# Retention attention and a top-1 expert layer on one core: expert weights loaded late and one at a time, and the work at the seam in a new order

## The chip, the cores and the metric

The kernel runs on one core of a Trainium2 chip. The core has TensorE (matmuls and transposes, into PSUM), VectorE, ScalarE and GpSimd for elementwise work, and SyncE, which here only issues transfers; 16 transfer engines are shared by all queues. The metric is the device time of one execution in microseconds, the median of three runs.

## The reference

For 8 batches, 8 heads, 576 tokens and a head size of 64 it computes retention (scores times a decay, causal, without softmax), puts the heads side by side to rows of 512, and sends each row through the one expert of eight that its gate picks:

```python
scores = scale * np.matmul(q, k.transpose(0, 1, 3, 2))
gamma = 1.0 - 2.0 ** (-5.0 - np.arange(H))
ret = scores * Dmat                     # gamma ** (i - j) for i >= j, else 0
attn = np.matmul(ret, v)
x = attn.transpose(0, 2, 1, 3).reshape(B * S, H * D)      # 4608 rows of 512
logits = x @ w_gate                                        # 8 experts
expert_idx = np.argmax(logits, axis=1)
gate_w = softmax(logits)[np.arange(N), expert_idx]
for e in range(E):
    mask = expert_idx == e
    h = np.maximum(x[mask] @ w1[e], 0.0)                   # 512 -> 1024
    out[mask] = gate_w[mask, None] * (h @ w2[e])           # 1024 -> 512
```

Everything comes and goes as float32.

## The kernel before

**Attention.** The tokens of a batch are cut into four blocks of 128 (c = 0 to 3) and one of 64 (c = 4), 40 blocks `i` in all. The main loop runs over them, and the order in which it is written is the order on every engine. The decay is put into k and q: `scale_k` and `scale_q` (mostly GpSimd) write `kk` and `qq`; `stage_T` transposes both on TensorE, ScalarE copies them to `kT` and `qT`. `stage_SC` makes a block's scores in the two PSUM tiles `pssc` as upper-triangle halves, and VectorE masks them into `sc`; `stage_S` adds a block to the running state `pss`, which `stage_se` copies to `se`; `stage_AV` (inside the block) and `stage_IN` (from the state) make the block's output in `psx`, which ScalarE copies to `xT` (line 429). `stage_xb` and `stage_R` turn it back to rows in bf16, and `put_rows` writes them to the DRAM tensor `x_rows`. A block's stages are spread over the loop: block `i` is scored while block `i+2` is transposed. SyncE issues, in the loop's order, k eight blocks ahead, v eight blocks ahead, q a batch ahead and the rows; a load waits for a mark of the loop (`after`) and for its buffer (`ldk` 6, `ldv` 8).

**Routing.** One batch later `stage_L1` and `stage_L2` make the gate's logits, and `route_batch` (VectorE, a generator that the loop advances by `steps`) finds each row's expert, its place among that expert's slots, and the gate weight, which `put_gates` and `write_gates` write beside the row. Each expert has 640 slots: `CA` of them (phase 0) for tokens of the first batches, `CB` (phase 1) for the others. `make_slots(0)` makes the lists of phase 0 as soon as half of the batches are placed, `make_slots(1)` the rest at the end.

**Experts.** A phase of an expert gathers its rows by indirect transfers of 128 rows (`gather`, GpSimd), transposes them (`trans`), multiplies by w1 (`mm1`, ReLU on ScalarE) and by w2 (`mm2`, times the gate on VectorE), and scatters 128 rows at a time to the output (GpSimd). The phases run as `seq`: phase 0 of the first `NA` experts, then their phase 1, then both phases of each further expert. After each ReLU or group of ReLUs, and after each scatter, `on` is called; the first calls carry the rest of the last batch's routing (`script`). Weights come in 64 parts of 0.52 MB, eight an expert, by casting transfers that GpSimd issues (`load_w`): `early` says how many at which block, and `fetch` takes the next ones. Five parts follow the attention loop, six come with the third phase and four with each phase after it. Experts below `EW` have buffers of their own; the others' buffers lie where the attention's were.

## Time and profile before

| what | value |
|---|---|
| median of 3 runs | 348.36 us (346.74 to 349.30) |
| profiled execution, its own time | 348.43 us |
| its span, first to last instruction | 346.7 us |
| mean granted clock of TensorE | 0.989 |
| busy: TensorE, ScalarE, GpSimd, VectorE | 314.7, 184.5, 201.0, 134.2 us |
| moved by the transfer engines | 65.98 MB, mean 190 GB/s |

The prediction sums against the profiled execution's own time, which is its span and what lies around it. The attention ends near 184 us, the experts fill the rest.

### The profile page before, as it was taken

How to read it: one execution, taken by the hardware profiler on the slowest of the kernel's cores; microseconds unless marked ns; L12 is line 12 of the kernel's file. 1: busy time of each engine (PE TensorE's matmuls, PEld its weight loads, DVE VectorE, ACT ScalarE, POOL GpSimd, SP SyncE). 2: the span in 40 equal slices, each digit the busy share in tenths (PEclk: the TensorE clock that was granted, in tenths of full speed). 3: DMA queues.
4: the chain of work that ended last, by engine and by line, in shares of the span. 5: the costliest groups of instructions: out<-in, count | busy, mean ns of one | idle time of the engine just before them, and what ended most of it. 6: DMA issues, size and time to landing. Idle time of an engine off the chain costs nothing. (4 is left out here: it accounts for less than half of the span.)

```text
span 346.7 us, 12050 instructions
## 1 busy us (share of the span) xinstructions
PE 314.7 (91%) x5099; PEld 231.4 (67%) x5115; DVE 134.2 (39%) x412; ACT 184.5 (53%) x371; POOL 201.0 (58%) x257
## 2 busy tenths in 40 slices
PE   6998999979989898997879998999999999999991
PEld 5777887768878787876767664455656465565650
DVE  5432446454564646654463622211212121221211
ACT  4467685655757667475555435355353535354440
POOL 3476755544445552647930287887886887865322
PEclk9999999999999999999998999999999999999997
DMA  8998989989999999996999159898999799953112
GB/s 206 216 236 206 245 204 212 253 202 242 218 227 223 232 225 219 253 198 145 190 203 182 44 145 215 187 207 187 229 200 211 139 208 222 208 163 117 58 58 79
DMA packets 117321, 65.98 MB, mean 190 GB/s; under 512 B 88590, under 2 KB 109582, under 8 KB 117264
## 3 DMA queue, kind: packets, MB, share of 16 engines
q0 software_dynamic: 18432, 31.80, 44.2%
q1 hardware_dynamic: 98304, 33.37, 41.5%
q8 instruction: 41, 0.67, 0.8%
q14 instruction: 16, 0.13, 0.1%
q10 hardware_dynamic: 528, 0.02, 0.1%
HBM read 67.45 MB, written 15.53 MB: 239 GB/s over the span
## 5 line engine op out<-in xcount | busy, mean ns | idle before, releaser
L757 ACT ACTIVATE ht<-pm 128x384 bf16<-128x384 f32 (+1 forms) x96 | 50.5, 527 | 58.7 <-PE pm L62 41.2
L290 POOL TENSOR_TENSOR kk<-kt,kg 128x512 f32<-128x512 f32 x39 | 40.8, 1046 | 59.4 <-PE pss L62 32.2
L62 PE MATMUL py<-w2b,ht 128*128 128x512 bf16 (+1 forms) x312 | 74.0, 374 | 1.1 <-DMA out_dram<-ys,tids 0.2
L62 PE MATMUL pm<-xt,w1b 128*128 128x256 bf16 (+1 forms) x512 | 73.1, 300 | 0.9 <-ACT xt L742 0.9
L915 DVE TENSOR_SCALAR ys<-py,gsl 128x512 f32<-128x512 f32 (+1 forms) x41 | 30.2, 737 | 105.1 <-PE py L62 76.1
L918 POOL DMA_INDIRECT out_dram<-ys,tids x40 | 40.9, 1022 | 48.5 <-DVE s L599 13.8
L62 PEld LDWEIGHTS <-w1b 128*128 128x128 bf16 x512 | 49.8, 98 | 23.3 <-issue 1.3
L384 DVE TENSOR_TENSOR sc<-pssc,mask 128x512 f32<-128x512 f32 x64 | 41.2, 685 | 28.9 <-PE pssc L62 26.6
L62 PEld LDWEIGHTS <-ht 128*128 128x128 bf16 x328 | 30.6, 98 | 30.5 <-ACT ht L757 1.1
L697 POOL DMA_INDIRECT xg<-x_rows,tidg x40 | 41.3, 1032 | 11.9 <-issue 11.2
L62 PE MATMUL psx<-sc,vt 128*64 128x128 f32 (+1 forms) x640 | 38.9, 265 | 1.2 <-issue 0.9
L62 PE MATMUL pssc<-qT,kT 64*64 64x64 f32 (+1 forms) x1024 | 36.1, 256 | 3.2 <-issue 1.7
L280 POOL TENSOR_TENSOR qq<-qt,qg 128x512 f32<-128x512 f32 x28 | 29.7, 1062 | 15.3 <-DMA qt<-in_q_dram 14.6
L323 ACT COPY kT<-pst 128x512 f32<-128x512 f32 x40 | 23.5, 587 | 22.3 <-PE pst L65 18.9
L429 ACT COPY xT<-psx 128x512 f32<-128x512 f32 x32 | 18.8, 587 | 30.1 <-PE psx L62 22.6
L742 ACT COPY xt<-pt 128x512 bf16<-128x512 bf16 x40 | 22.8, 587 | 20.3 <-PE pt L65 12.1
L62 PEld LDWEIGHTS psx<-sc,vt 128*64 128x64 f32 (+1 forms) x640 | 30.8, 136 | 2.5 <-issue 1.6
L62 PEld LDWEIGHTS pssc<-qT,kT 64*64 64x64 f32 x1024 | 27.6, 133 | 7.0 <-ACT xr L475 2.9
L475 ACT COPY xr<-pssc 128x512 bf16<-128x512 bf16 (+1 forms) x38 | 22.6, 596 | 9.6 <-PE pssc L65 9.5
L258 POOL DMA_DIRECT2D w2b<-in_moe_w_dram x32 | 24.3, 781 | 3.0 <-DMA w2b<-in_moe_w_dram 2.3
L62 PE MATMUL pss<-vt,kk 128*64 128x64 f32 x512 | 22.7, 227 | 2.2 <-issue 2.2
L62 PEld LDWEIGHTS pss<-vt,kk 128*64 128x64 f32 x512 | 18.1, 137 | 4.4 <-issue 2.6
(128 smaller groups left out, 373.9 us busy)
## 6 DMA issues: line engine op xcount, KB each, us to landing
kt<-in_k_dram SPq DMA_DIRECT2D x32, 256.0 KB, 5.5
qt<-in_q_dram SPq DMA_DIRECT2D x16, 512.0 KB, 5.5
vt<-in_v_dram SPq DMA_DIRECT2D x32, 256.0 KB, 5.4
w1b<-in_moe_w_dram POOLq DMA_DIRECT2D x32, 256.0 KB
w2b<-in_moe_w_dram POOLq DMA_DIRECT2D x32, 256.0 KB
x_rows<-xr SPq DMA_DIRECT2D x32, 128.0 KB, 5.4
kt<-in_q_dram SPq DMA_DIRECT2D x8, 128.0 KB, 5.7
kt<-in_k_dram SPq DMA_DIRECT2D x8, 128.0 KB, 4.8
```

The source lines that it names most:

```text
L62: nc.tensor.matmul(out=out, lhsT=lhsT, rhs=rhs, start=start, stop=stop, skip_group_check=True)
L258: after(nc.gpsimd.dma_start(out=wb[e][part // n][:, o:o + m, :], in_=w[e, o * P:(o + m) * P, :].rearrange("(c p) f -> p c f", p=P)), dep)
L280: eng.tensor_tensor(out=qq[:, :, :].rearrange("p s (h d) -> p h s d", d=DH), in0=qts[b][:, h0:h0 + 2, :, :], in1=qg[:, 0:NCH, h0:h0 + 2].r ...
L290: eng.tensor_tensor(out=kk[:, :, :], in0=kts.pop(i)[:, :, :], in1=kg[:, blocks[i][1], :].unsqueeze(2).to_broadcast([P, H, DH]), op=ALU.mult)
L323: mark["kT"] = nc.scalar.copy(out=kT[:, :, :].rearrange("p a (u t) -> p u a t", u=2), in_=ps[:, :, o:o + 256].rearrange("p u (a t) -> p u ...
L384: mark["sc"] = nc.vector.tensor_tensor(out=sc[:, j, :, :], in0=pssc[j][:, :].rearrange("p (a i) -> p a i", i=P), in1=mask[:, :].unsqueeze( ...
L475: nc.scalar.copy(out=xr[0:m, :].rearrange("p (a t) -> p a t", t=P), in_=ps)
L697: nc.gpsimd.indirect_dma_start(out=xg[:, :], out_offset=None, in_=x_rows[0:nr, :], in_offset=bass.IndirectOffsetOnAxis(ap=slots[ph][1][:, ...
L742: nc.scalar.copy(out=xts[(e, ph)][:, :, j * P:(j + 1) * P], in_=pt[:, :, :])
L757: nc.scalar.activation(out=ht[:, f0:f0 + per, :], in_=pm[:, :, :], func=AF.Relu)
L915: nc.vector.tensor_scalar(out=ys[:, r], in0=py[:, r], scalar1=gsl[:, e, slots[ph][2] + j:slots[ph][2] + j + 1], scalar2=None, op0=ALU.mult)
L918: scatters.append(nc.gpsimd.indirect_dma_start(out=next(outs)[:, :], out_offset=bass.IndirectOffsetOnAxis(ap=slots[ph][0][:, e, j:j + 1], ...
```

## The change

- **Sizes.** Phase 0 takes 384 slots of the first five batches (`BA`) instead of 256 of the first four, phase 1 has 256 instead of 384; `NA` and `EW` go from 3 to 2.
- **Loads at the start.** The first 128 rows of q of batch 0 are loaded and transposed alone (`qc0`, `first_TQ`); the other 384 rows come after k(1) and v(0); batch 1's q comes after the second block's scores and is scaled and transposed in the last two blocks of batch 0, in part on VectorE and through `scr`. q of later batches is issued at c = 0 and 2 instead of 1 and 3, ahead of k. k is loaded nine blocks ahead and v seven (seven buffers each).
- **Scores.** A batch's first block is scored in full 128 by 128 tiles, and the clearing of `pssc` at the start is gone.
- **Order.** At c = 4 the copies `stage_se` and `stage_xb` come behind the scores and the output stage. One row copy (`NB - 3`) goes to VectorE.
- **Weights.** Nothing is loaded before the last batch; there one part comes with each block, five after the loop, one with each of the calls 0 to 5, and then one with every second call from 8 on. Of experts 2 to 7 the four parts of w2 are loaded by SyncE as float32 into a staging tile, each behind the last ReLU, and cast by VectorE eight or more calls later.
- **Second layer's rows.** w2 parts are read so that a partition holds two neighbouring rows. The first layer's columns are taken with a step of two to match.
- **Routing and seam.** The gathers of phase 0 come one a block from the second block of the last batch on; the last batch's gates are computed and written sooner; gate writes of the last three batches cover exactly their own rows; the script's steps lie at calls 0, 1, 2, 4 and 8, and one of expert 0's transposes lies inside `stage_L1`. GpSimd drains once before the last expert.

```diff
-CA = 256
-CB = 384
+CA = 384
+CB = 256
...
-NA = 3
-EW = 3
+NA = 2
+EW = 2
+BA = 5
...
-    ldk = p1.enter_context(tc.tile_pool(name="ldk", bufs=6))
-    ldv = p1.enter_context(tc.tile_pool(name="ldv", bufs=8))
+    ldk = p1.enter_context(tc.tile_pool(name="ldk", bufs=7))
+    ldv = p1.enter_context(tc.tile_pool(name="ldv", bufs=7))
...
+    qc0 = attc.tile([P, H, DH], F32, name="qc0")
     load_k(0)
-    load_q(0, 0)
-    load_q(0, 1)
-    for i in range(5):
-        load_k(i + 1)
-        load_v(i)
-        if i % 2:
-            load_q(1, i // 2)
+    nc.sync.dma_start(out=qc0[:, :, :], in_=q[0, :, 0:P, :].rearrange("h p d -> p h d"))
+    load_k(1)
+    load_v(0)
+    qts[0] = ldq.tile([P, H, NCH, DH], F32, tag="q", name="qt")
+    for g in range(2):
+        hs = slice(g * NP, (g + 1) * NP)
+        nc.sync.dma_start(out=qts[0][:, hs, 0:NCH - 1, :],
+                          in_=q[0, hs, P:NCH * P, :].rearrange("h (p s) d -> p h s d", p=P))
+    load_k(2)
+    load_v(1)
+    load_k(3)
+    load_v(2)
+    load_k(4)
...
-                                  in_=w[e, o * P:(o + m) * P, :].rearrange("(c p) f -> p c f", p=P)), dep)
+                                  in_=w[e, o * P:(o + m) * P, :].rearrange(
+                                      "(c p) f -> p c f" if part < n else "(p c) f -> p c f", p=P)), dep)
...
+            n = 1 if c == 0 else 2
             for p in range(NP):
-                for u in range(2):
+                for u in range(n):
                     for j in range(2):
                         r = slice(j * DH, (j + 1) * DH)
-                        mm(pssc[j][u * DH:(u + 1) * DH, p * P + u * DH:(p + 1) * P], kT[r, p, u * DH:(u + 1) * DH],
+                        m = slice(u * P // n, (u + 1) * P // n)
+                        mm(pssc[j][m, p * P + u * DH:(p + 1) * P], kT[r, p, m],
                            qT[r, p, c * P + u * DH:(c + 1) * P], True, True)
...
+            if a == 1:
+                between()
...
+        if b == B - 1:
+            yield from gates(b, ex)
+            put_gates(b)
...
-        if b == B // 2:
+        if b == BA:
...
+        n = NCOL if b < B - 3 else NCH
+        o = x_rows[b * S:b * S + n * P, DW:XW].rearrange("(t p) u -> p t u", p=P)
+        todo_g.append((o, gat[:, b * NCOL:b * NCOL + n, :]))
+        if n < NCOL:
+            todo_g.append((x_rows[b * S + n * P:(b + 1) * S, DW:XW], gat[0:REM, b * NCOL + n, :]))
...
-        per = 2 if ph == 0 else 1
+        per = 512 // n
...
-                    mm(pm[:, o, :], w1b[:, c, fb * P:(fb + 1) * P], xt[:, c, :], c == 0, c == NPT - 1)
-            nc.scalar.activation(out=ht[:, f0:f0 + per, :], in_=pm[:, :, :], func=AF.Relu)
+                    mm(pm[:, o, :], w1b[:, c, fb // 2 * 2 * P + fb % 2:fb // 2 * 2 * P + 2 * P:2], xt[:, c, :],
+                       c == 0, c == NPT - 1)
+            mark["mm"] = nc.scalar.activation(out=ht[:, f0:f0 + per, :], in_=pm[:, :, :], func=AF.Relu)
...
-    early = {i: 1 if i < NB - NCOL else 2 for i in (*range(10, 32, 3), *range(NB - NCOL - 1, NB))}
-
-    def fetch(n):
+    early = {NB - 5: 1, NB - 4: 1, NB - 3: 1, NB - 2: 1, NB - 1: 1}
+
+    staged = []
+
+    def fetch(n, call=0):
         for e, j in [wq.pop(0) for _ in range(min(n, len(wq)))]:
-            load_w(e, j, 4, wpool if e < EW else wpool2)
+            if e < EW or j < 4:
+                load_w(e, j, 4, wpool if e < EW else wpool2)
+            else:
+                st = stg.tile([P, 2, DM], F32, tag="st", name="st")
+                after(nc.sync.dma_start(out=st[:, :, :], in_=moe_w2[e, (j - 4) * 2 * P:(j - 3) * 2 * P, :]
+                                        .rearrange("(p c) f -> p c f", p=P)), mark["mm"])
+                staged.append((call, e, j - 4, st))
+
+    def cast_staged(call):
+        if staged and staged[0][0] + 8 <= call:
+            _, e, j, st = staged.pop(0)
+            nc.vector.tensor_copy(out=wb[e][1][:, 2 * j:2 * j + 2, :], in_=st[:, :, :])
...
+        if b == B - 1 and c > 0:
+            gather_first(1)
         fetch(early.get(i, 0))
-        load_k(i + 8, mark.get("sc"))
-        stage_T(i + 2, b + 1, c - 1 if c > 0 and b + 1 < B else None)
-        if c in (1, 3) and b + 2 < B:
-            load_q(b + 2, c // 2, mark.get("kT"))
+        if c in (0, 2) and b + 2 < B:
+            load_q(b + 2, c // 2, mark.get("sc"))
+        load_k(i + 9, mark.get("sc"))
...
+        if c < NCH or i == NB - 1:
+            stage_se()
...
+        if c == NCH and i < NB - 1:
+            stage_se()
+            stage_xb(i - 1)
+        load_v(i + 7, mark.get("xT"))
...
+    gather_first(len(first))
+    fetch(5)
...
-    script = [lambda: stage_L2(B - 1), lambda: (stage_R(NB - 1), put_rows()), turn, None, turn,
-              None, None, None, turn, lambda: make_slots(1)]
+    script = {0: lambda: stage_L2(B - 1), 1: turn, 2: lambda: (stage_R(NB - 1), put_rows()), 4: turn,
+              8: lambda: (turn(), make_slots(1))}
+    calls = iter(range(1000))
     last.append(True)
 
     def on(i):
 
-        f = script.pop(0) if script else None
-        if f:
-            f()
+        n = next(calls)
+        script.get(n, lambda: None)()
         write_gates()
         gather_upto(i + 2)
+        cast_staged(n)
+        if n < 6 or n > 7 and n % 2 == 0:
+            fetch(1, n)
...
+    stg = p2.enter_context(tc.tile_pool(name="stg", bufs=5))
...
-        fetch((EW * 8 - sum(early.values()), 0, 6)[i] if i < NA else 4)
...
+        if i == len(seq) - 2:
+            nc.gpsimd.drain()```

Three places show the new order. First SyncE at the start of the program, before and then after (`kt`, `vt`, `qt` are k, v and q in SBUF, `qc` the single piece of q; of a row the shape is partitions by the rest):

```order
L121 DMA kt<-in_k_dram 128x8x64
L115 DMA qt<-in_q_dram 128x4x256 x2
L121 DMA kt<-in_k_dram 128x8x64
L121 DMA vt<-in_v_dram 128x8x64
L121 DMA kt<-in_k_dram 128x8x64
L121 DMA vt<-in_v_dram 128x8x64
L115 DMA qt<-in_q_dram 128x4x256
L121 DMA kt<-in_k_dram 128x8x64
L121 DMA vt<-in_v_dram 128x8x64
L134 DMA kt<-in_q_dram 64x8x64
```

```order
L122 DMA kt<-in_k_dram 128x8x64
L153 DMA qc_118<-in_q_dram 128x8x64
L122 DMA kt<-in_k_dram 128x8x64
L122 DMA vt<-in_v_dram 128x8x64
L159 DMA qt<-in_q_dram 128x4x192 x2
L122 DMA kt<-in_k_dram 128x8x64
L122 DMA vt<-in_v_dram 128x8x64
L122 DMA kt<-in_k_dram 128x8x64
L122 DMA vt<-in_v_dram 128x8x64
L135 DMA kt<-in_q_dram 64x8x64
```

The rest of the first q moved behind k(1) and v(0), and the half of the second batch's q (the seventh row before) is gone from this stretch.

Second GpSimd in the third batch's blocks, before and then after (`kk` and `qq` are the scaled k and q):

```order
L258 DMA w1b<-in_moe_w_dram 128x1024
L280 TENSOR_TENSOR qq<-qt,qg 128x2x4x64
L290 TENSOR_TENSOR kk<-kt,kg 128x512
L280 TENSOR_TENSOR qq<-qt,qg 128x2x4x64
L290 TENSOR_TENSOR kk<-kt,kg 128x512
L280 TENSOR_TENSOR qq<-qt,qg 128x2x4x64
L290 TENSOR_TENSOR kk<-kt,kg 128x512
L258 DMA w1b<-in_moe_w_dram 128x1024
```

```order
L299 TENSOR_TENSOR qq<-qt,qg 128x2x4x64
L309 TENSOR_TENSOR kk<-kt,kg 128x512
L299 TENSOR_TENSOR qq<-qt,qg 128x2x4x64
L309 TENSOR_TENSOR kk<-kt,kg 128x512
L299 TENSOR_TENSOR qq<-qt,qg 128x2x4x64
L309 TENSOR_TENSOR kk<-kt,kg 128x512 x2
```

The weight parts, one every third block, are gone from between the scalings.

Third GpSimd from the end of the attention into the first experts, before and then after (`xg` are gathered rows, `out_dram` scatters, `tidg` the gather lists of the two phases):

```order
L258 DMA w2b<-in_moe_w_dram 128x2x512 x3
L258 DMA w1b<-in_moe_w_dram 128x1024 x4
L258 DMA w2b<-in_moe_w_dram 128x2x512 x4
L918 DMA out_dram<-ys,tids_3139 4608x512 x2
L697 DMA xg<-x_rows,tidg_4290 128x272 x3
L918 DMA out_dram<-ys,tids_3139 4608x512 x2
L258 DMA w1b<-in_moe_w_dram 128x1024 x4
L258 DMA w2b<-in_moe_w_dram 128x2x512 x2
L697 DMA xg<-x_rows,tidg_4290 128x272 x3
```

```order
L762 DMA xg<-x_rows,tidg_3528 128x272 x2
L272 DMA w2b<-in_moe_w_dram 128x1024 x3
L272 DMA w1b<-in_moe_w_dram 128x1024 x4
L272 DMA w2b<-in_moe_w_dram 128x1024 x4
L1035 DMA out_dram<-ys,tids_3527 4608x512
L762 DMA xg<-x_rows,tidg_4175 128x272 x2
L272 DMA w1b<-in_moe_w_dram 128x1024
L1035 DMA out_dram<-ys,tids_3527 4608x512 x2
L272 DMA w1b<-in_moe_w_dram 128x1024
L762 DMA xg<-x_rows,tidg_4175 128x272 x2
```

The gathers of phase 1 moved ahead of the second scatter, and the six weight parts that stood together ahead of the next gathers became single ones; w2 is no longer among them.

## Rows read from the trace of the kernel before

**Rows 1.** The page, parts 1 and 2: busy time, and DMA in 40 slices.

```profile
PE 314.7 (91%) x5099; PEld 231.4 (67%) x5115; DVE 134.2 (39%) x412; ACT 184.5 (53%) x371; POOL 201.0 (58%) x257
...
DMA  8998989989999999996999159898999799953112
```

**Rows 2.** Busy time by stretch (us from the span's start, cut at xT copies).

```profile
core 0: us, PE busy (x) PEld busy (x) DVE busy (x) ACT busy (x) POOL busy (x), PEclk, DMA share, GB/s
36.20:55.78 19.58, 19.08 (x511) 16.45 (x515) 11.18 (x35) 13.74 (x30) 12.64 (x18) 1.00 0.98 222
55.78:79.36 23.58, 20.19 (x516) 16.84 (x520) 11.69 (x37) 13.73 (x29) 12.03 (x13) 1.00 0.96 219
79.36:100.77 21.41, 19.77 (x516) 16.84 (x520) 11.63 (x36) 13.73 (x29) 9.81 (x10) 1.00 1.01 228
100.77:121.21 20.44, 19.26 (x516) 16.66 (x520) 11.63 (x36) 13.74 (x30) 10.76 (x11) 1.00 1.06 232
121.21:141.87 20.66, 19.37 (x516) 16.75 (x520) 12.41 (x40) 13.73 (x30) 10.04 (x11) 1.00 0.99 220
141.87:166.11 24.24, 21.17 (x529) 17.60 (x533) 11.73 (x36) 13.73 (x30) 14.54 (x17) 1.00 0.90 200
166.11:184.68 18.57, 15.81 (x374) 13.28 (x370) 11.04 (x37) 10.65 (x22) 10.06 (x14) 0.92 1.11 195
184.68:234.49 49.81, 46.95 (x329) 28.93 (x330) 15.74 (x56) 22.70 (x43) 31.31 (x36) 0.99 0.77 161
234.49:328.52 94.03, 92.14 (x611) 56.42 (x620) 20.28 (x50) 45.23 (x85) 66.85 (x75) 1.00 0.81 178
328.52:346.70 18.18, 10.64 (x64) 6.16 (x63) 3.22 (x5) 3.93 (x8) 4.18 (x5) 0.88 0.18 67
```

**Rows 3.** Timeline of GpSimd: two of the eight weight parts in the loop.

```profile
51.52 0.77 POOL L258 DMA_DIRECT2D w1b<-in_moe_w_dram  x1
...
64.16 0.61 POOL L258 DMA_DIRECT2D w1b<-in_moe_w_dram  x1
```

**Rows 4.** Timeline of the start, in order of time.

```profile
4.02 0.69 DVE L290 TENSOR_TENSOR kk<-kt,kg 128x512 f32<-128x512 f32 x1 [0.63 <-DMA kt<-in_k_dram]
...
10.78 1.27 PE L62 MATMUL pssc<-qT,kT 64*64 64x128 f32 x32
...
15.10 1.09 PE L62 MATMUL pssc<-qT,kT 64*64 64x128 f32 x32
...
15.65 1.04 POOL L290 TENSOR_TENSOR kk<-kt,kg 128x512 f32<-128x512 f32 x1 [2.85 <-DMA kt<-in_k_dram]
...
19.24 1.04 POOL L290 TENSOR_TENSOR kk<-kt,kg 128x512 f32<-128x512 f32 x1 [1.52 <-DMA kt<-in_k_dram]
...
36.20 0.59 ACT L429 COPY xT<-psx 128x512 f32<-128x512 f32 x1 [0.81 <-PE pss L62]
```

**Rows 5.** The page, part 3, and groups by line of GpSimd's issues.

```profile
q0 software_dynamic: 18432, 31.80, 44.2%
...
L697 POOL DMA_INDIRECT xg<-x_rows,tidg x40 | 41.3, 1032 | 11.9 <-issue 11.2
...
L258 POOL DMA_DIRECT2D w2b<-in_moe_w_dram x32 | 24.3, 781 | 3.0 <-DMA w2b<-in_moe_w_dram 2.3
...
L258 POOL DMA_DIRECT2D w1b<-in_moe_w_dram x32 | 19.0, 625 | 0.0
```

**Rows 6.** Timeline of TensorE among the experts.

```profile
217.38 0.40 PE L65 MATMUL pt<-identb,xg 128*128 128x128 bf16 x4 [2.00 <-DMA xg<-x_rows,tidg]
...
320.90 3.66 PE L62 MATMUL pm<-xt,w1b 128*128 128x256 bf16 x32
...
328.52 5.36 PE L62 MATMUL pm<-xt,w1b 128*128 128x384 bf16 x32
```

**Rows 7.** Weight loads of TensorE: a group by line, and a timeline row.

```profile
L62 PEld LDWEIGHTS <-w1b 128*128 128x128 bf16 x512 | 49.8, 98 | 23.3 <-issue 1.3
...
8.05 1.36 PEld L65 LDWEIGHTS scr<-ident 128*128 128x128 f32 x7
```

**Rows 8.** Groups by line: VectorE's longest bf16 write from f32.

```profile
L640 DVE TENSOR_TENSOR rh<-scr,r 128x640 bf16<-128x640 f32 x8 | 6.3, 784 | 0.0
```

## What the change was predicted to do

> **What bounds the kernel now.** I read the page first, then the span cut at its stages. The page [rows 1] shows one engine near full all the way: TensorE is busy for 314.7 of 346.7 us, every other engine for less than 60%. The slices below show that the transfer engines are just as full for the first two thirds: DMA stands at 8 or 9 tenths in nearly every slice while the attention runs, falls to 1 in the slice from 191 us, and fades after 310 us. So there are two bounds, and the cut [rows 2] tells which holds where.
>
> The first six rows of [rows 2] run from the copy of a batch's first block to that of the next batch's. In each TensorE has the same 516 matmuls to do (511 and 529 records at the two ends), so equal work takes 19.58, 23.58, 21.41, 20.44, 20.66 and 24.24 us. In the shortest TensorE is busy for 19.08 us, in the others for 19.26 to 21.17 with more idle time; DMA is at 0.90 to 1.06 and 200 to 232 GB/s in all six. Attention is thus held by both: TensorE can do a batch in some 19.2 us, and the transfers add what they add. A batch moves q, k and v (3.54 MB) and its rows (0.59 MB), 4.13 MB, 18.6 us at the 222 GB/s of the first row. What comes on top are weights for the experts, a part every 12 us or so [rows 3].
>
> The experts are different. From 234.49 to 328.52 us TensorE is busy for 92.14 of 94.03 us [rows 2], five experts at 18.81 us each, and DMA has 0.81. Nothing but fewer matmuls would shorten that. Ahead of the batches lies a start that waits for loads; between batches and experts a seam (166.11 to 234.49): in its first part TensorE idles 2.8 us and has a granted clock of 0.92, so some of it runs at 1.2 instead of 2.4 GHz, and in its second DMA is not full (0.77).
>
> The span splits into 36.20 (start) + 129.91 (six batches) + 18.57 (last batch and seam) + 49.81 (first experts) + 94.03 + 18.18 = 346.70 us. The profiled execution took 348.43 us, 1.73 more than its span, and lies at the median of the three runs (348.36), so I sum against it. About 1% is what a measurement of this kernel tells from no change.
>
> **The start.** Before, SyncE queues all of the first batch's q behind k(0), and the next batch's q in two halves among the first batch's blocks. GpSimd's scaling of k(3) and k(4) waits for its load by 2.85 and 1.52 us [rows 4]. The first scores begin at 10.78 us, the second block's at 15.10, and the first block of the second batch is copied at 36.20. After, a q piece of 128 rows is loaded alone, so the first scores need 0.52 MB and not 1.3. But the second block's scores still need k(0), all of q, k(1) and v(0) in front of them: 1.83 MB, 8.3 us at 222 GB/s. k(0), 0.26 MB, was in use at 4.02 us, 2.8 us after such a rate would have it, so the last q lands near 11.1 us; a scaling (1.06 on GpSimd), transposes (0.4) and two copies (0.59 each) put the second scores at some 13.4-13.7 us. From there the old kernel needed 21.1 us to the copy at 36.20. Half of the next batch's q (0.52 MB, 2.4 us of transfers) has left the queue ahead of k(3), so the wait of 2.85 us falls to 0.45; the wait of 1.52 for k(4) follows a scaling of q that has left these blocks too, and I halve it. The next batch's q is now transposed in two blocks instead of four, half of it by whole tiles: 0.8 us more. That gives 21.1 - 2.4 - 0.8 + 0.8 = 18.7, and with 13.6 the copy at 32.3 us: **-3.9**. Bounds: -1.5 (only the earlier scores count) and -6 (the added 0.8 lies beside other work, and both waits go whole).
>
> **The six batches.** Eight weight parts leave the loop (blocks 10 to 31, every third); none comes in. What a part costs the transfers: the queue that GpSimd feeds (q0) has 44.2% of 16 engines' span, 153.2 us, for 64 parts and 80 indirect transfers [rows 5]. The last 18.18 us hold five scatters and almost nothing else, at a share of 0.18 [rows 2]: 3.3 us, 0.65 each. 80 of them are 52 us, and (153.2 - 52)/64 = 1.58 us a part, an estimate. Two parts in a batch are 3.2 us over 18.6 us that TensorE's 19.2 nearly equals. The one row that had almost no weight in it (its only part was issued at 51.52, 4 us before its end [rows 3]) took 19.58 us; the next five averaged 22.07. The sixth of them also had four of the gathers and three of its four parts issued by GpSimd at its end. I take 19.8 a batch, just above the row without weights: 118.8, **-11.1**. Lower bound 19.2 (TensorE's own work), -14.7; upper bound 21.1, the mean of the first five as they are, -3.3. The smaller edits fall in here: the first block's scores in 8 full matmuls instead of 16 halves, q issued two blocks sooner and ahead of k, and the copies at the fifth block behind the scores, so that VectorE no longer waits for ScalarE there. Together they may give 0.2 us a batch, which I leave inside the 19.8. k is loaded one block further ahead and v one block less; at 3.9 us a block seven blocks are 27 us of lead, and I cost that at nothing.
>
> **Last batch and seam.** Weights start in the last batch, one a block, and gathers with them, one a block from the second on; GpSimd has no scaling left by then and runs on without TensorE, so the sixteen parts of the first two experts are all issued before the eighth call of the first expert: at 0.6 to 0.8 us each plus six gathers of 1.03, about 17 us of issuing. TensorE is idle for 2.8 of 18.57 us there [rows 2]. Expert 0's last transpose now lies inside the router's matmuls, one row copy has moved to VectorE. I take **-0.6** (0 to -1.5).
>
> **The first experts.** Phase 0 is now 384 tokens of five batches for two experts, not 256 of four for three: before the late tokens are needed TensorE has two phases of 11 us instead of three of 7.6, some 22 us in both cases. The second gather list is made at the ninth call instead of the tenth, and calls in a 384 phase are shorter (0.65 us against 0.9), some 4 us sooner. Before, TensorE waited 2.00 us for a gather that stood behind six weights issued together [rows 6]; single weights and the earlier list take that away. The routing's own matmuls stay. **-1.5** (+1.5 to -3). Largest fill of an expert, counted from the inputs: 619 of 640 slots, so the slow branch stays shut.
>
> **Steady experts and end.** 40 blocks, the same matmuls; 0. Two things are new. The first layer's weights are read with a step of two columns, 512 loads. No row shows such a load. The packed ones are listed at 98 ns each [rows 7] and hide under the matmuls, which run every 114 ns at 256 columns and some 165 at 384 (3.66 and 5.36 us for 32 [rows 6]); the dearest loads of 128 columns are f32 ones, seven in 1.36 us, 194 each [rows 7]. So the ends are 0 and 256 x (194 - 114) + 256 x (194 - 165) = +27.9 us. I take 0, because the step moves the same 128 two-byte elements and the nearest row by type is the packed one. The Trainium skill, *TensorE: Matmul & The Clock Gate*, on weight-path modes, says the fast load holds for column steps up to 1,024 elements; by that the sum stays, and no run here shows it yet. The other new thing: 24 parts of the second layer come by SyncE as f32 and VectorE casts them, 128x1024 each. The nearest VectorE row is 128x640 f32 to bf16 in 784 ns [rows 8]: 1.25 us each, four an expert, 5 us of VectorE's 18.81, where it is busy for 20.28 of 94.03 us now [rows 2]. An eviction waits for a cast at most 1.25 us; there are two output banks and 1.95 us a block, so TensorE does not see it. GpSimd loses 24 issues of 0.78 us [rows 5].
>
> **Sum.** 32.3 + 118.8 + 18.0 + 48.3 + 94.0 + 18.2 = 329.6, with 1.73 outside the span **331.3 us**.
>
> **Rivals.** *The pace is not the weights'.* q, k, v and rows alone fill 18.6 us, and shares of 0.96 to 1.06 do not follow the weights (two parts in the 23.58, two in the 20.44). Then batches stay at 21.1: 348.4 - 3.9 - 3.3 - 2.1 = 339. Chance 0.16. *Late weights become the wait.* From the ninth call 48 parts come in 94 calls of 1.106 us, 104 us (17 calls an expert); they and some 55 indirect transfers need 48 x 1.58 + 55 x 0.65 = 112. The transfers then end 8 us late, a cast waits for its part, and the evictions behind it on VectorE hold TensorE: 339. Chance 0.11. *Stepped columns are slow to load*, slower than before: it decides once a load takes more than some 173 ns, where both matmul widths have eaten the 17 us; at 194 ns 359 us. Chance 0.07. *GpSimd becomes the bound*: the casts hold it off. It has 4 x 0.62 + 10 x 1.03 = 12.8 us of issuing an expert, 17.8 with the casts added, which fits in 18.81; only casts of twice that price make it late, 4 us an expert for six: 355. Chance 0.03. The rule behind that one is the Trainium skill's, *SBUF — State Buffer*, where an f32 copy on VectorE keeps GpSimd from writing descriptors; no row here shows or denies it.
>
> **How the numbers follow.** Forecast (322 to 338) 0.60, the rivals 0.16, 0.11, 0.07, 0.03, unseen harm 0.03. Lower bounds together: 348.4 - 6 - 14.7 - 1.5 - 3 = 323.2. Upper: 348.4 - 1.5 - 3.3 + 1.5 = 345.1. I say 322 to 345. Faster by over 1% (under 344.9) 0.83, within 1% 0.07, slower 0.10.
>
> **What would show it.** The second batch's first copy near 32 us; batches of 19 to 20 us with DMA below 0.97; no wait of TensorE for a gather; the first layer's loads still near 98 ns; 18.8 us an expert. Wrong if batches stay above 21 us, if VectorE's casts wait for transfers, or if the first layer's 32 matmuls take over 5.5 us at 256 columns.

## The result, and the profile after

The changed kernel takes 328.53 us (median) against 348.76 for the kernel before on the same chip: a ratio of 0.9425, 95% interval 0.9366 to 0.9484. The prediction was 331.3 us in a range of 322 to 345. The profiled execution took 328.53 us, 1.73 more than its span, as before. The chip now and then has a slower spell in which a run takes over 1.5% longer than the kernel's fastest; the ratios leave such runs out, but the profiles of five experiments (weights back in the loop, weights late and single, the old split, no drain, all second-layer parts by GpSimd) are of such runs.

The page of the changed kernel, parts 1 and 2, against [rows 1]:

```profile
PE 310.5 (95%) x4965; PEld 231.5 (71%) x4981; DVE 152.6 (47%) x437; ACT 184.1 (56%) x371; POOL 185.1 (57%) x235
...
DMA  9999998899998999965999499999999999973121
```

TensorE is busy for 4.2 us less, in a span 19.9 us shorter: most of what went away is its idle time, 32.0 us before and 16.3 now.

The span of the changed kernel cut as in [rows 2], but the experts cut where an expert ends (three, then five), then the last scatter:

```profile
core 0: us, PE busy (x) PEld busy (x) DVE busy (x) ACT busy (x) POOL busy (x), PEclk, DMA share, GB/s
34.52:54.46 19.94, 18.90 (x495) 16.61 (x499) 11.18 (x35) 13.81 (x29) 12.93 (x21) 1.00 1.02 225
54.46:74.93 20.47, 19.41 (x500) 16.92 (x504) 11.76 (x37) 13.81 (x29) 9.24 (x9) 1.00 0.96 239
...
134.29:153.50 19.21, 19.09 (x503) 16.82 (x506) 11.86 (x39) 13.71 (x29) 8.60 (x9) 1.00 0.72 161
153.50:170.69 17.19, 15.24 (x388) 12.78 (x385) 11.64 (x41) 10.07 (x20) 13.14 (x20) 1.00 0.95 183
170.69:229.62 58.93, 57.27 (x391) 34.88 (x394) 25.03 (x72) 28.44 (x55) 36.99 (x42) 1.00 0.97 248
229.62:322.28 92.66, 91.34 (x607) 56.48 (x615) 32.00 (x65) 43.06 (x82) 55.59 (x58) 1.00 0.74 224
322.28:326.80 4.52, 0.00 (x0) 0.00 (x0) 0.00 (x0) 0.00 (x0) 0.98 (x1) 0.81 0.23 86
```

The same cut of the experts of the kernel before, which [rows 2] cuts elsewhere:

```profile
184.68:245.31 60.63, 57.72 (x391) 34.86 (x394) 18.11 (x61) 27.70 (x53) 39.70 (x46) 1.00 0.79 165
245.31:340.01 94.70, 92.02 (x611) 56.65 (x619) 21.13 (x50) 44.17 (x83) 61.66 (x68) 1.00 0.72 165
340.01:346.70 6.69, 0.00 (x0) 0.00 (x0) 0.00 (x0) 0.00 (x0) 0.98 (x1) 0.67 0.17 59
```

The differences, as measured and as predicted: start -1.7 (-3.9); six batches 118.98 for 129.91, -10.9 (-11.1); last batch and seam -1.4 (-0.6); first three experts -1.7 (-1.5); five experts -2.0 (0); end -2.2 (0). Their sum is -19.9 and takes 346.7 to 326.8. More than half of the gain is in the batches. The six in one row, before and after:

```profile
36.20:166.11 129.91, 118.85 (x3084) 101.15 (x3088) 70.28 (x219) 82.40 (x175) 69.83 (x78) 1.00 0.98 220
```

```profile
34.52:153.50 118.98, 115.22 (x2978) 100.91 (x2981) 70.01 (x217) 82.46 (x174) 58.48 (x66) 1.00 0.94 218
```

What TensorE waits for there stands in its list of waits, first for the kernel before and then for the changed one, both over the six batches (sum, times, longest):

```profile
PE pssc L65 <- issue: 2.3, 2, 1.2
PE pss L62 <- issue: 2.2, 3, 0.9
PE pssc L62 <- ACT xr L475: 1.3, 6, 0.2
PE pssc L62 <- issue: 1.2, 4, 0.4
```

```profile
PE psx L63 <- issue: 1.5, 3, 0.6
PE pst L66 <- issue: 1.1, 2, 0.7
PE pssc L63 <- ACT xr L529: 0.5, 2, 0.3
```

"issue" is a wait for which the profile names nobody. It falls from 7.6 us (all such rows of the six batches summed) to 2.6. GpSimd, too, waits less for q, first before and then after:

```profile
POOL qq L280 <- DMA qt<-in_q_dram: 14.6, 7, 3.8
```

```profile
POOL qq L299 <- DMA qt<-in_q_dram: 2.0, 2, 1.1
POOL kk L309 <- DMA qt<-in_q_dram: 2.7, 1, 2.7
```

Which part of the change did that could not be read from this pair. Two rows of the changed kernel settle what the prediction had priced without a row, the loads with stepped columns and the casts:

```profile
L63 PEld LDWEIGHTS <-w1b 128*128 128x128 bf16 x512 | 49.8, 98 | 21.5
...
L889 DVE CAST w2b<-st 128x1024 bf16<-128x1024 f32 x24 | 17.7, 740 | 16.6 <-DMA st<-in_moe_w_dram 12.8
```

The stepped loads take the 98 ns of the packed ones [rows 7], and a cast 0.74 us on the mean. VectorE waits 12.8 us for parts to cast, while the list of TensorE's waits has one row among the experts:

```profile
PE pt L66 <- DMA xg<-x_rows,tidg: 1.3, 1, 1.3
```

### The profile page after: what moved, and what is told of

Read it like the earlier page. It is cut to its first block, busy times and chain, and to the rows that moved or that the text cites. A ratio compares the mean times of both kernels' runs of the same rounds, so it can differ in the third digit from the quotient of the medians.

```text
span 326.8 us, 11831 instructions
## 1 busy us (share of the span) xinstructions
PE 310.5 (95%) x4965; PEld 231.5 (71%) x4981; DVE 152.6 (47%) x437; ACT 184.1 (56%) x371; POOL 185.1 (57%) x235
## 2 busy tenths in 40 slices
DMA  9999998899998999965999499999999999973121
## 3 DMA queue, kind: packets, MB, share of 16 engines
q0 software_dynamic: 10880, 25.50, 32.3%
## 5 line engine op out<-in xcount | busy, mean ns | idle before, releaser
L309 POOL TENSOR_TENSOR kk<-kt,kg 128x512 f32<-128x512 f32 x39 | 41.0, 1053 | 65.9 <-issue 37.5
L63 PE MATMUL py<-w2b,ht 128*128 128x512 bf16 (+1 forms) x312 | 73.6, 374 | 0.8
L63 PE MATMUL pm<-xt,w1b 128*128 128x384 bf16 (+1 forms) x512 | 72.8, 299 | 0.0
L1035 POOL DMA_INDIRECT out_dram<-ys,tids x40 | 42.3, 1058 | 45.0 <-DVE ys L1032 18.1
L63 PEld LDWEIGHTS <-w1b 128*128 128x128 bf16 x512 | 49.8, 98 | 21.5
L63 PEld LDWEIGHTS <-ht 128*128 128x128 bf16 x328 | 30.8, 98 | 29.8
L762 POOL DMA_INDIRECT xg<-x_rows,tidg x40 | 42.0, 1050 | 15.2 <-issue 7.3
L63 PE MATMUL psx<-sc,vt 128*64 128x128 f32 (+1 forms) x640 | 38.7, 266 | 1.4 <-issue 1.1
L63 PE MATMUL pssc<-qT,kT 64*64 64x128 f32 (+2 forms) x896 | 36.7, 262 | 0.1
L299 POOL TENSOR_TENSOR qq<-qt,qg 128x512 f32<-128x512 f32 (+1 forms) x28 | 29.2, 1044 | 6.8 <-DMA qt<-in_q_dram 4.9
L63 PEld LDWEIGHTS psx<-sc,vt 128*64 128x64 f32 (+1 forms) x640 | 30.7, 136 | 2.7 <-issue 1.5
L63 PEld LDWEIGHTS pssc<-qT,kT 64*64 64x64 f32 (+1 forms) x896 | 29.0, 143 | 3.0 <-issue 0.5
L889 DVE CAST w2b<-st 128x1024 bf16<-128x1024 f32 x24 | 17.7, 740 | 16.6 <-DMA st<-in_moe_w_dram 12.8
L529 ACT COPY xr<-pssc 128x512 bf16<-128x512 bf16 (+1 forms) x37 | 22.0, 594 | 3.1 <-PE pssc L66 2.9
L63 PE MATMUL pss<-vt,kk 128*64 128x64 f32 x512 | 22.0, 229 | 0.0
L66 PE MATMUL pst<-ident,kk 64*128 64x64 f32 x320 | 19.0, 237 | 1.7 <-issue 0.7
```

The source lines that it names most:

```text
L63: nc.tensor.matmul(out=out, lhsT=lhsT, rhs=rhs, start=start, stop=stop, skip_group_check=True)
L66: nc.tensor.transpose(out=out, in_=in_, identity=identity)
L299: eng.tensor_tensor(out=qq[:, 0:n, :].rearrange("p s (h d) -> p h s d", d=DH), in0=qts[b][:, h0:h0 + 2, 0:n, :], in1=qg[:, o:o + n, h0:h0 ...
L309: eng.tensor_tensor(out=kk[:, :, :], in0=kts.pop(i)[:, :, :], in1=kg[:, blocks[i][1], :].unsqueeze(2).to_broadcast([P, H, DH]), op=ALU.mult)
L529: nc.scalar.copy(out=xr_out, in_=ps)
L762: nc.gpsimd.indirect_dma_start(out=xg[:, :], out_offset=None, in_=x_rows[0:nr, :], in_offset=bass.IndirectOffsetOnAxis(ap=slots[ph][1][:, ...
```

## The experiments

My theory: the eight weight parts in the loop cost the batches their time, and they had to be late and single so as not to cost it again. The rivals: the reordered loads did it; late weights are harmless however they come; the end is the drain's. An experiment's ratio is to the kernel before; where one is said to be slower than the changed kernel, the number is the difference of the two ratios times 348.76 us. Stretches are read from one profile each. How far one profile goes is seen from four kernels below that have the changed kernel's loop as it stands: their six batches take 118.89 (bursts), 117.89 (the swap at the start), 118.56 (all by GpSimd) and 122.17 us (no drain), for 118.98.

**Weights back in the loop.** The changed kernel with eight of its sixteen parts among the blocks again.

```diff
-    early = {NB - 5: 1, NB - 4: 1, NB - 3: 1, NB - 2: 1, NB - 1: 1}
+    early = {i: 1 for i in (*range(10, 32, 3), *range(NB - 5, NB))}
...
-    fetch(5)
+    fetch(3)
...
-        if n < 6 or n > 7 and n % 2 == 0:
+        if n > 7 and n % 2 == 0:
```

> The changed kernel with eight of its first sixteen weight parts put back among the attention blocks (one at every third block from 10 to 31), three in place of five behind the loop, and none with the first six first-layer calls; everything else as changed. Theory (weight transfers set the pace of the batches): the four batches that hold the eight parts go from 19.9 back to about 21.5 us each, so the six take 125 to 127 us where they took 119.0, and the time is 335 to 337 us. Rival (the reordered edits in the loop set the pace): the batches stay within 1 us of 119.0 and the time is 328 to 330 us.

Ratio to the kernel before 0.9569 (0.9464 to 0.9673): some 5 us slower than the changed kernel, with intervals that overlap a little. Its two runs behind the ratio took 330.27 and 332.90 us, less than the 335 to 337 expected. The six batches took 126.37 us, within the theory's range, but in a profile of 335.94 us, and unevenly: one batch of 27.17, the others at 18.77 to 20.86. That did not settle it, so the dose was doubled.

**All sixteen parts in the loop.**

```diff
-    early = {NB - 5: 1, NB - 4: 1, NB - 3: 1, NB - 2: 1, NB - 1: 1}
+    early = {i: 1 for i in range(8, 40, 2)}
...
-    fetch(5)
...
-        if n < 6 or n > 7 and n % 2 == 0:
+        if n > 7 and n % 2 == 0:
```

> The changed kernel with all sixteen first weight parts among the attention blocks, one at every second block from 8 to 38, none behind the loop and none with the first six calls: twice the eight that were put back before. Theory 1 (with q asked for sooner the transfers are hidden): undisturbed batches stay at 19.2 to 20.2 us, the time is 328 to 331 us, and if anything the experts start better. Theory 2 (the weights' bytes set the pace whatever the order): five batches hold about three parts each and take 22 to 23 us, time 341 to 345 us.

Ratio 0.9843 (0.9773 to 0.9914), 14.6 us slower than the changed kernel. The batches took 132.23 us, five of them 21.4 to 23.9: theory 2. Their row, and the waits of TensorE and one of GpSimd over them:

```profile
34.43:166.66 132.23, 115.58 (x2975) 100.87 (x2979) 70.31 (x219) 82.80 (x174) 66.09 (x79) 1.00 0.99 219
...
PE pst L66 <- issue: 5.7, 5, 1.7
PE pss L63 <- issue: 5.0, 2, 3.0
PE pss L63 <- DMA vt<-in_v_dram: 4.6, 6, 1.6
...
POOL qq L299 <- DMA qt<-in_q_dram: 32.6, 12, 5.0
```

The unnamed waits are back at 10.7 us, and v and q land late. The batches are 13.25 us longer than the changed kernel's. Of the sixteen parts 14 are issued within the six batches (the last two behind them), where the changed kernel issues one: 13 more, 1.02 us each, about two thirds of the 1.58 us that the prediction estimated for one in the transfers.

**The kernel before, weights late and nothing else.**

```diff
-    early = {i: 1 if i < NB - NCOL else 2 for i in (*range(10, 32, 3), *range(NB - NCOL - 1, NB))}
+    early = {i: 1 if i < NB - NCOL else 2 for i in range(NB - NCOL - 1, NB)}
```

> The kernel before with one edit alone: the eight weight parts among blocks 10 to 31 are left out of the loop and issued in one burst with the five that stood behind the first first-layer calls (thirteen there). Theory (their transfers set the pace): the six batches go from 129.9 to about 119 to 121 us and the time is 338 to 340 us, if the burst delays nothing. Rival 1 (order edits set the pace): batches stay at 129 to 130 us, time 348. Rival 2 (late weights in a burst become the wait): batches 120 us, but first experts lengthen by 5 us or more, and the time is 343 us or above.

Ratio 1.0034 (0.9991 to 1.0076): nothing. The batches fell to 122.16 us (-7.75, or 0.97 for each of the eight parts), close to what the theory says, with unnamed waits of 2.3 us; and the stretch from the first first-layer matmul on grew from 162.0 to 170.8 us, so rival 2 took all of it back. The row of the batches, and what TensorE waited for behind them, gathers that stood behind the burst:

```profile
36.68:158.84 122.16, 116.34 (x3071) 100.15 (x3075) 70.43 (x219) 82.36 (x174) 61.13 (x66) 1.00 0.90 211
...
PE pt L65 <- DMA xg<-x_rows,tidg: 5.9, 3, 2.7
PE pss L62 <- DVE gsl L741: 2.7, 1, 2.7
```

**The kernel before, weights late and single.**

```diff
+        n = next(calls)
+        if n < 13 or n > 15 and n % 2 == 0:
+            fetch(1)
...
-        fetch((EW * 8 - sum(early.values()), 0, 6)[i] if i < NA else 4)
```

(with `early` as in the run above, the first lines at the end of `on`, and a counter `calls` as in the changed kernel)

> The kernel before with late weights as in the run of that name, but singly: thirteen parts one by one at the first thirteen calls among the experts, the rest one at every second call from the sixteenth on, none in a burst. Theory (the burst gave the gain of the batches back): batches as with the burst, 122 us or a little less, the experts back from 170.8 to 161 to 163 us, time 338 to 341 us. Rival (with three experts' weights due early, lateness itself is what costs): experts 167 us or more, time 345 to 348 us.

Ratio 1.0093 (1.0045 to 1.0142): slower than before, and slower than the rival's 345 to 348 us; my theory fell here. The profile (of a run of 357.10 us, the median is 354.37) has TensorE wait for the weights themselves from the first experts on:

```profile
PE pm L62 <- DMA w1b<-in_moe_w_dram: 4.7, 4, 2.0
PE py L62 <- DMA w2b<-in_moe_w_dram: 2.6, 1, 2.6
```

Three experts' weights, 24 parts, are due within 18 short calls; issued singly they are late. The attention loop is that of the run above, yet its batches took 131.17 us in this profile: four at 19.60 to 20.23, two at 26.80 and 24.77. Why these two are long no run shows, and it is a reason not to lean on the 122.16 us of a single profile to the tenth.

**The changed kernel with the old split.** Three experts first, on four batches; weights stay late and single.

```diff
-CA = 384
-CB = 256
+CA = 256
+CB = 384
...
-NA = 2
-EW = 2
-BA = 5
+NA = 3
+EW = 3
+BA = 4
...
-        if n < 6 or n > 7 and n % 2 == 0:
+        if n < 14 or n > 15 and n % 2 == 0:
```

> The changed kernel with the split of the experts as before the change: three experts in place of two start on the rows of the first four batches in place of five, with 256 rows in place of 384, and come back for 384 in place of 256; the weights stay late and single (one at each of the first fourteen calls, then one at every second). Theory 1 (sixteen parts due early in place of twenty-four are what makes lateness harmless): TensorE waits for weights or gathers, experts 161 us or more where the changed kernel has 156.1, time 333 to 340 us; the end behind the last scatter 6.5 to 6.9 us with the longer last pass. Theory 2 (single weights are enough): 156 to 158 us, time 328 to 330 us; the end 4.3 to 4.6 us.

Ratio 0.9871 (0.9813 to 0.9929), 15.6 us slower than the changed kernel: theory 1, by more than it had (343.11 us for 333 to 340). Its waits of TensorE among the experts, and its busy time where they lie (the profiled run took 348.49 us, 5 more than the median):

```profile
PE py L63 <- DMA w2b<-in_moe_w_dram: 7.0, 3, 3.7
PE pm L63 <- DMA w1b<-in_moe_w_dram: 3.7, 2, 2.8
```

```profile
190.00:205.00 15.00, 8.36 (x31) 4.09 (x31) 1.68 (x5) 1.18 (x2) 11.09 (x13) 0.66 1.01 200
```

TensorE is busy for 8.36 of 15 us while the transfers are full (1.01). Behind its idle time the granted clock is 0.66 in the stretch, so much of what it does there runs at 1.2 and not at 2.4 GHz. With 24 parts due early TensorE waits for weights, with sixteen it does not: late weights go with two experts first. (Slots, batches and experts of the first phase went back together; which of them counts most was not taken apart.) The end behind the last scatter was 4.9 us with the long last pass, not 6.5 to 6.9.

**Bursts in place of single parts.** The changed kernel, from the experts' calls on.

```diff
-        if n < 6 or n > 7 and n % 2 == 0:
-            fetch(1, n)
+        if n == 0 or n > 7 and n % 8 == 0:
+            fetch(4 if n else 6, n)
```

> The changed kernel with its weight parts from the experts' calls on in bursts: six at the first call in place of one at each of six, then four at every eighth call in place of one at every second. Nothing else differs, attention does not. Theory (what the kernel before loses when its parts come late is the burst ahead of the gathers): TensorE waits for gathers again, 4 to 6 us in sum between the first first-layer matmul and the third pass, time 332 to 335 us. Rival (six parts are few enough, and what matters is that sixteen in place of twenty-four stand there): no gather wait over the 1.3 us of the changed kernel, time 328 to 329.5 us.

Ratio 0.9576 (0.9518 to 0.9635), 5.3 us slower: the size is the theory's, the place only in part. TensorE lists no wait for a gather; VectorE does, 4.4 us in the third pass. TensorE idles for 3.3 us there, of which the profile puts 2.4 down to nobody and 0.9 to ScalarE; that it stands behind VectorE's evictions is likely but not shown. That pass is 4.1 us longer, and the transfers are full in it:

```profile
196.70:209.66 12.96, 9.65 (x58) 5.37 (x57) 4.35 (x10) 3.34 (x6) 8.97 (x10) 0.87 1.02 325
```

Experts 2 to 6 took 18.61, 18.80, 20.69, 18.45 and 18.44 us, each from its first first-layer matmul to that of the next; in the changed kernel all five lie at 18.44 or 18.45, in the kernel before experts 3 to 6 at 18.45, 19.59, 19.11 and 18.44. Two late experts, 1.8 us above the others, are most of the 2.0 us that the steady experts gained, and bursts bring more than that back. The slowest of the kernel before, and the one before it:

```profile
245.31:263.76 18.45, 18.34 (x124) 11.28 (x124) 4.06 (x10) 9.04 (x17) 14.30 (x17) 1.00 1.03 217
263.76:283.35 19.59, 18.63 (x123) 11.27 (x124) 3.97 (x10) 9.14 (x17) 15.69 (x19) 1.00 0.90 190
```

**The order of the q loads undone.** The changed kernel with q again behind k, two blocks later and waiting for the k transposes.

```diff
-        if c in (0, 2) and b + 2 < B:
-            load_q(b + 2, c // 2, mark.get("sc"))
         load_k(i + 9, mark.get("sc"))
         stage_T(i + 2, b + 1, qp[0] if qp else None)
+        if c in (1, 3) and b + 2 < B:
+            load_q(b + 2, c // 2, mark.get("kT"))
```

> The changed kernel with the order of the q loads alone undone (second and fourth block, behind k, waiting for the k transposes); the copies of a last block stay behind its scores. Theory 1 (the 124.1 us of the run with both undone are q's): batches 123 to 125 us and 30 us or more of GpSimd waiting for q, time 335 to 338 us. Theory 2 (they are the copies'): batches 119 to 120 us, 328 to 330 us.

Ratio 0.9778 (0.9719 to 0.9837), 12.3 us slower than the changed kernel; the batches took 127.25 us (+8.3), the start and the experts stayed:

```profile
34.74:161.99 127.25, 118.20 (x2988) 103.03 (x2992) 70.81 (x219) 82.56 (x175) 60.47 (x68) 0.99 0.86 206
```

Theory 1 by the times, though GpSimd's wait for q was only 7.8 us in this profile, not 30 or more.

**The same, and the copies of the fifth block ahead of the scores again.**

```diff
-        if c < NCH or i == NB - 1:
-            stage_se()
-            stage_xb(i - 1)
+        stage_se()
+        stage_xb(i - 1)
...
-        if c == NCH and i < NB - 1:
-            stage_se()
-            stage_xb(i - 1)
```

(q as in the run above)

> The changed kernel with two of its reorderings in the attention loop undone: the copies of a last block's states stand ahead of its scores again, and the q loads come at the second and fourth block behind k and wait for the k transposes. Theory (they are worth little, 0.2 us a batch): six batches 119 to 121 us, time 328.5 to 330 us. Rival (what is left between the kernel before without weights in its loop, 122.2 us, and the changed one, 119.0 us, is theirs): 122 us or more, time 331.5 to 333 us.

Ratio 0.9655 (0.9573 to 0.9737), 8.0 us slower than the changed kernel; batches 124.08 us (+5.1), above the rival's 122. Their row, and GpSimd's first row of waits there:

```profile
34.69:158.77 124.08, 115.29 (x2975) 100.67 (x2979) 69.41 (x219) 82.33 (x174) 58.60 (x66) 1.00 0.86 206
...
POOL qq L299 <- DMA qt<-in_q_dram: 37.4, 10, 4.7
```

It is no slower than with q's order alone undone, so the copies' place is worth nothing that these runs can tell. Putting q back costs 5.1 to 8.3 us of batches in the two profiles, 8.0 to 12.3 by the ratios.

**The kernel before, q sooner and nothing else.**

```diff
+        if c in (0, 2) and b + 2 < B:
+            load_q(b + 2, c // 2, mark.get("sc"))
         load_k(i + 8, mark.get("sc"))
         stage_T(i + 2, b + 1, c - 1 if c > 0 and b + 1 < B else None)
-        if c in (1, 3) and b + 2 < B:
-            load_q(b + 2, c // 2, mark.get("kT"))
```

> The kernel before with one edit alone: the q loads two blocks ahead stand at the first and third block, ahead of that block's k load, and wait for the scores, where they stood at the second and fourth behind it and waited for the k transposes. The eight weight parts stay in the loop. Theory 1 (q that lands late is how the full queues reach TensorE, and order alone cures it): six batches from 129.9 to 120 to 122 us, time 339 to 341 us. Theory 2 (the weights' bytes set the pace, as the prediction had it): batches 128 to 130 us, time 347 to 350 us. Between: 124 to 126 us, both have a part.

Ratio 1.0095 (1.005 to 1.014), batches 132.35 us: a little worse, as neither theory had it. GpSimd no longer waits for q, but for k, which stands behind it (0.3 us before):

```profile
37.57:169.92 132.35, 118.57 (x3082) 100.93 (x3086) 71.34 (x219) 82.34 (x174) 68.55 (x77) 1.00 0.94 212
...
POOL kk L290 <- DMA kt<-in_k_dram: 39.7, 17, 6.0
```

Here the order only chose who was late. The changed kernel asks for k a block sooner as well and has no weights there; which of the two makes q's new place pay was not taken apart.

**The scores of the second block sooner.**

```diff
-    stage_AV(0)
-    stage_IN(0)
-    stage_SC(1)
+    stage_SC(1)
+    stage_AV(0)
+    stage_IN(0)
```

> The changed kernel with the scores of the second block ahead of the first block's values product in the code that starts the pipeline. Theory A (the start ends with those scores, as the prediction took it): they begin at 14.0 us where they began at 15.06, and the second batch's first copy comes at 33.5 in place of 34.52, time 327.5 us. Theory B (from 11 us on TensorE is busy without a gap and the sum of its work sets the end of the start): the scores come sooner by 1 us, the copy at 34.3 to 34.8, time 328.5 us. A step back, if the values product was what was waited for: copy at 35 or later.

Ratio 0.9438 (0.9381 to 0.9494): the same as the changed kernel. The scores began at 12.63 us, 2.4 sooner, and the copy came at 34.58, as theory B had it. One of the 2.4 us is the order; q's last transposes, which go ahead either way, also came sooner (12.29 us for 13.57). At 20 us TensorE was still some 1.2 us ahead of the changed kernel, and gave it back in waits for what GpSimd scales:

```profile
23.40 0.46 PE L66 MATMUL pst<-ident,kk 64*128 64x64 f32 x8 [0.32 <-POOL kk L309]
24.42 0.46 PE L66 MATMUL pst<-ident,qq 64*128 64x64 f32 x8 [0.56 <-POOL qq L299]
```

In the changed kernel GpSimd scales this q at 22.21 us, here at 23.31, behind a k that it scaled at 18.35 (17.25 there) after waiting 3.0 us for its load. TensorE transposes the q at 24.42 us here and at 24.52 there, without a wait. So in this profile the lead was lost to a load that came late, and not to the sum of TensorE's work; the six runs show no gain either way.

**No drain.** The line `nc.gpsimd.drain()` ahead of the last two passes left out.

> The changed kernel without the wait of GpSimd for its outstanding transfers ahead of the last two passes. Theory (the drain takes over part of what the end waits for): from the last scatter issue to the end of the span 6.5 to 6.9 us as before the change, where it is 4.5 us with it; time 330.3 to 331 us. Rival (the shorter end is from the lighter queues, or chance): 4.3 to 4.8 us, time 328.5 us; if the drain held up something, up to 1 us faster.

Ratio 0.9497 (0.9422 to 0.9572), not to be told from the changed kernel; 4.4 us from the last scatter to the end in its profile. The drain is not what shortened the end.

**All second-layer parts by GpSimd.**

```diff
-            if e < EW or j < 4:
+            if True:
```

> The changed kernel with all second-layer weight parts issued by GpSimd and cast in the transfer, none staged by SyncE and cast by VectorE (24 parts change their way; the interleaved rows stay). Theory (an expert is bound by TensorE either way): steady experts stay at 18.4 to 18.8 us, the time is 328 to 330 us. Rival 1 (24 issues of 0.78 us on GpSimd, 19 us in the stretch, hold gathers and scatters back): TensorE waits for gathers again, 332 to 336 us. Rival 2 (the casts on VectorE cost something): 326 to 327.5 us.

It has no ratio: its four runs took 327.43, 333.02, 333.30 and 334.99 us. The profile (333.30 us) has 156.03 us from the first first-layer matmul to the end (156.11 in the changed kernel), six batches of 118.56, steady experts at 18.44 with one of 18.53. In this one profile, staging by SyncE and the casts neither gain nor cost anything that shows among the experts.

No ratio is below the changed kernel's.

## Why the prediction was right, and where not

**Six batches.** -11.1 forecast, -10.9 measured; the mechanism was most of it, not all. Weights in the loop cost what the step said in kind: eight parts out of the kernel before give -7.75 us, thirteen more within the changed one's batches +13.25. That is 0.97 to 1.02 us a part, and leaves 3.2 of the 10.9 to the other edits of the loop. The step that failed is "together they may give 0.2 us a batch" for them: it is 0.5. The order of the q loads is one of them, and undoing it alone costs more than all of them are worth together, 5.1 to 8.3 us. The parts do not add up: the new order gains nothing while weights fill the queues, the old order does less harm in the kernel before without weights (122.2 us) than in the changed one (124.1 and 127.3). What else differs between those two loops, k loaded nine blocks ahead and v seven, the first block's scores in full tiles, no run took apart. I had taken the best row of [rows 2] as the target; late weights alone average 20.4 us a batch, so that the 19.8 came out is in part luck. DMA below 0.97 came on the mean (0.94 for 0.98) and in three of the six batches (0.96, 0.87, 0.72), the others are at 1.02 and 1.03.

**Start.** The mis-sized term: -3.9 forecast, -1.7 measured. The scores of the second block came at 15.06 us, not 13.6, because the last transposes of q and the first block's values product went ahead of them. The swap shows that this alone was not the error: scores at 12.63 us did not move the copy, though there a late k took the lead back. The step that failed is the path: I ran it from those scores, and did not sum what TensorE has to do. It is busy for 31.44 us up to the copy (30.26 before), so 32.3 would have left it 0.9 us of idle time; from 20.20 to 34.52 us it is busy for all of 14.32 us. That this work is what holds the start is argued from these numbers; no run with less of it was made.

**Last batch, seam and first experts.** -0.6 and -1.5 forecast, -1.4 and -1.7 measured; but a gather still holds TensorE once, 1.3 us where it was 2.00 [rows 6]. The reason given, single parts and an earlier list, was incomplete. The old split with single parts is 15.6 us slower: the two-expert split, which I had set at nothing ("some 22 us in both cases"), is what this term needs.

**Steady experts and end.** 0 and 0 forecast, -2.0 and -2.2 measured. I read 18.81 us an expert as TensorE's own; it was 18.44 with two late experts among them, and bursts bring such experts back. The end is shorter in all kernels built on the changed one (4.3 to 4.9 us), without the drain and with the old split too. In the profile of the transfers the last bytes move some 3.0 us behind the last scatter's issue before and 2.6 after; most of the difference is the rest, some 3.7 and 1.9 us in which nothing moves. What shortens it stays open.

**The rivals.** *Late weights become the wait* was right as a mechanism: it eats the whole gain in the kernel before, in bursts or singly. Here it did not decide, and the old split points to the reason that I had not weighed, sixteen parts due early instead of 24. Its first step came, too, and I had named it as a sign of being wrong: VectorE's casts wait for transfers, 12.8 us in sum. The second did not: TensorE's list has no wait for VectorE. *The pace is not the weights'* was right for less than a third of the term, as said. *Stepped columns* fell with 98 ns; the Trainium skill, *TensorE: Matmul & The Clock Gate*, on weight-path modes, has the fast load hold for such steps, and the row agrees. *GpSimd becomes the bound* fell too: in the changed kernel a scatter is issued in 1,058 ns on the mean, in the kernel without casts in 1,025. The casts do touch the issues beside them:

```profile
196.45 0.69 DVE L889 CAST w2b<-st 128x1024 bf16<-128x1024 f32 x1 [0.32 <-ACT ht L823]
196.60 1.44 POOL L1035 DMA_INDIRECT out_dram<-ys,tids  x1 [0.30 <-issue]
```

Of 24 gathers and scatters whose issue overlaps a cast, 12 took more than 1.10 us, up to this 1.44; of the others among the experts none took more than 1.07. The Trainium skill, *SBUF — State Buffer*, on the two separate sides (the "DVE blocks DMA" trap), has an f32 copy on VectorE keep GpSimd from writing descriptors; the trace agrees in kind, at 33 ns a scatter on the mean.

The errors of the terms (+2.2, +0.2, -0.8, -0.2, -2.0, -2.2) add up to -2.8 us, which is 331.3 against 328.5: the start's error and those of the experts and the end cancel in part, so the sum is luckier than its terms.

## What to carry to other kernels

Bytes moved out of a full stretch came back here as a wait where they were due next: count what is due early there, and cut that (fewer experts first) before the move, or the gain is given back in full. In these batches the order of the loads was worth about as much as the bytes, but neither shortened the kernel alone, so test such changes both apart and together. A wait that names nobody is a symptom to count.

## What the runs showed that I had not expected

- With weight parts among the batches TensorE stands longer in waits without a releaser. Over the six batches these sum to 7.6 us (before), 7.5 and 10.7 (parts put back, eight and all sixteen), 11.0 (q sooner on the kernel before), against 1.4 to 2.7 in eight of the ten kernels without weights there (4.9 and 5.2 in the other two). The transfers' share is 0.98 before and 0.94 after, so it is not fullness alone. What such a wait is for, no run shows.
- A cast of 128x1024 from f32 to bf16 takes 0.68 to 0.97 us, 0.74 on the mean; my 1.25 came from a comparison with broadcast operands, 128x640 in 784 ns [rows 8].
- The first block's scores, 16 matmuls of 64x128, took 2.08 us at 7.72 us, and the same form 1.16 us at 30.16. The swap's run has them at 7.55 us in 1.16, and the granted clock is 1.00 there in both, so neither the place nor the clock explains it; why is open.
